# Float16 upper part of the attention weights and the sums' shift on ScalarE, the mixing matmul a step ahead, and the reciprocal last in VectorE's step

## Chip, cores and metric

The kernel runs on one core of a Trainium2 chip. The metric is the time of one execution on the device in microseconds (us); for a version that was run several times it is the median of its runs.

## What is computed

Attention with two mixings over its twelve heads, and a feed-forward part behind it. Cut to what matters (`B, H, S, D = 4, 12, 448, 64`; 1792 tokens, model width 768, inner width 2048):

```python
scores = (1 / sqrt(D)) * q @ k.T                    # each batch and head
scores = einsum('bhij,hg->bgij', scores, w_pre)     # mixing over heads
attn = exp(scores - max(scores, axis=-1))
attn = attn / (sum(attn, axis=-1) + 1e-9)
attn = einsum('bhij,hg->bgij', attn, w_post)        # mixing over heads
x = (attn @ v)                                      # rows: tokens, columns: heads x D
h = x @ w_in
out = (h * 1 / (1 + exp(-1.702 * h))) @ w_out
```

## The kernel before

Large operands are held as two float16 parts, an upper part and what the upper part leaves over (lower part), and a product takes three float16 matmuls. The arithmetic of q, k, v, of the weights and of the attention weights is scaled by powers of two for this.

The program is written out as a main loop of *steps*; a schedule fixed by the program's own order, each engine running its queue in that order. A step treats ten query rows of one batch with all twelve heads, 120 partitions x 448 keys; there are 45 steps for a batch, 180 in all, and behind them the rest of the feed-forward part. In the code `i` is the step.

- `scores` (L221) multiplies q and k for 120 query rows of a pair of heads, `keep_scores` (L231, on ScalarE or VectorE) copies the result out as `sc`, and SP's queue stores it to memory as `sd`. These come some 16 steps ahead (table `at_scores`). `gather(i)` (L247, SP's queue) reads the rows of one step back as `r`, all heads of ten query rows, `AHEAD` steps before.
- `mix(i)` (L257): one matmul in float32 (listed as two records), `mx`, two buffers in PSUM. `peak(i)` (L264, VectorE): the row maximum `nm`. `expo(i)` (L271, ScalarE): `e`, with the row sum `sm`; it comes in the trace with an accumulator read.
- `inverse(i)` (L280, L283, VectorE): `rs`, the scaled inverse of the sum: `sm` has a constant added and is scaled, then the reciprocal. `weigh(i)` (L289, GpSimd): `e` times `rs`, in place. `upper(i)` (L296, VectorE): the float16 part `a1`. `lower(i)` (L302, GpSimd): what is left, `a2`. (The trace names both `a`.)
- `post(i)` (L315 to L317): the second mixing, twelve matmuls into `pp`, `LAG` = 3 steps later. `keep_upper` (L331, ScalarE) and, a step after it, `keep_lower` (L334, VectorE) make the two parts `p`. `context` (L350) multiplies them with v; `x_upper`, `x_lower`, `x_size` make `x`.
- Feed-forward: its 384 *blocks* of six matmuls each (the `quanta`: `hidden`, L522, and `project`, L561) come between the steps' matmuls, 2.15 per step once `x` of the first batch is there. A block's results are taken by `gate` (L540 to L550) and `collect` (L578 to L591), on ScalarE and VectorE, with additions on GpSimd (L588). Matmuls of scores and blocks share three PSUM buffers.
- The weights come as 64-bit floats. `convert` makes sixteen blocks of them into float16 pairs, three parts each: five integer and float operations on VectorE (`magnitude` L423, `least` L427, `shift` L431, `rest` L437, `sign` L443), a sum of squares on ScalarE (L96), a small matmul that adds over partitions (`add_all`, L108), column operations, `w_upper` (L469, ScalarE) and `w_lower` (L472, VectorE), then a store to memory (`wd`). `fetch_w` (L510) reads a block back as `wt` for each use. `q`, `k`, `v` of later batches are treated in a like way (L96, L98, L180 to L188).

What decides where the movable work stands is a count of *tokens* for ScalarE ("A"), VectorE ("D") and GpSimd ("G"): each step adds 4.3 (5.2 when feed-forward blocks run), up to a limit of 3.0, and each operation takes its cost away. A conversion is put into a step only when its engine has tokens left; score copies, some squares and a block's collection go to ScalarE or VectorE, whichever has more. A block of weights has to be converted and stored before feed-forward blocks that read it are put in.

## Time and profile before

| | |
|---|---|
| median of 3 runs | 1174.65 us (1172.79 to 1176.52) |
| profiled execution | 1174.68 us |
| its span, first to last instruction | 1173.0 us |
| TensorE (matmuls) busy | 948.0 us, 81%, mean granted clock 0.886 |
| VectorE busy | 778.0 us, 66% |
| ScalarE busy | 567.3 us, 48% |
| GpSimd busy | 514.5 us, 44% |

The profile is of one execution. Busy time is the time in which an engine ran an instruction. Matmuls overlap each other, so a busy TensorE is not one at its peak. The granted clock is a share of full speed, 2.4 GHz; the lower level is 1.2 GHz, and figures between are means of the two. In rows, PE is TensorE, PEld its weight loads, DVE VectorE, ACT ScalarE, POOL GpSimd, SP the queue that issues most transfers; L is the line of the kernel.

### The profile page before, as it was taken

The page shows a single profiled execution, that of the slowest core. Times are in us where ns is not written, and L with a number is a line of the kernel's source. Part 1 is how long each engine was busy: PE and PEld are TensorE (multiplying, and loading weights), DVE is VectorE, ACT ScalarE, POOL GpSimd, SP SyncE. Part 2 cuts the span into 40 slices and gives each one's busy share as a digit, 9 for nine tenths or more (in the row PEclk, how much of TensorE's full clock was granted, in tenths as well). Part 3 has the DMA queues.
Part 4 walks back from the last instruction along what each step waited for, and adds up shares of the span by engine and source line. Part 5 has one row for each costly group of instructions (what it writes and reads, how often), then busy time and mean ns, then how long its engine had stood idle before and what let it go on. Part 6 is the DMA issues. An engine that isn't in the chain of part 4 may idle for free.

```text
span 1173.0 us, 21128 instructions
## 1 busy us (share of the span) xinstructions
PE 948.0 (81%) x7768; PEld 554.8 (47%) x7768; DVE 778.0 (66%) x1855; ACT 567.3 (48%) x1284; POOL 514.5 (44%) x463
## 2 busy tenths in 40 slices
PE   2557576685778987776659499899999999999998
PEld 1234344353445544443435256465555566555554
DVE  5788778778787878775875477555666566433333
ACT  4444654554546645643544355555544555332322
POOL 0355436545534556454643236455554456320111
PEclk9776768677689998987869799899999999999999
DMA  6766676655747756465644674644655532324332
GB/s 192 226 194 196 229 235 196 217 177 167 216 144 237 231 170 200 142 203 166 201 149 116 208 244 153 194 151 143 196 157 162 177 118 83 101 98 174 108 108 75
DMA packets 67436, 201.02 MB, mean 171 GB/s; under 512 B 7764, under 2 KB 32468, under 8 KB 67332
## 3 DMA queue, kind: packets, MB, share of 16 engines
q1 hardware_dynamic: 66928, 199.59, 53.9%
q8 instruction: 61, 1.00, 0.4%
q14 instruction: 43, 0.35, 0.1%
q10 hardware_dynamic: 404, 0.09, 0.0%
HBM read 143.02 MB, written 56.62 MB: 170 GB/s over the span
## 4 chain that ended last, share of the span: by engine, by line
PE 45%; DVE 29%; ACT 11%; DMA 9%; issue 4%; SPq 1%; ACTq 0%; POOL 0%; DVEq 0%
PE po L561 16%; PE h L522 15%; DVE p L334 5%; PE mx L257 5%; ACT e L271 4%; DVE nm L264 4%; ACT p L331 3%; PE av L350 3%; DVE w_f L437 3%; DVE w_f L443 3%; DMA wt<-wd 2%; DVE w_p L472 2%; DVE w_f L427 2%; DMA wd<-w_p 2%; PE qk L221 2%
## 5 line engine op out<-in xcount | busy, mean ns | idle before, releaser
L302 POOL TENSOR_TENSOR a<-e,a 120x448 f16<-120x448 f32 x180 | 193.4, 1074 | 365.7 <-DVE a L296 307.7
L561 PE MATMUL po<-g,wt 128*128 128x448 f16 x1152 | 248.3, 361 | 30.7 <-DMA wt<-wd 9.9
L289 POOL TENSOR_SCALAR e<-e,rs 120x448 f32<-120x448 f32 x180 | 212.5, 1180 | 127.9 <-DVE rs L283 118.6
L522 PE MATMUL h<-x,wt 128*128 128x448 f16 x1152 | 243.9, 357 | 21.9 <-DMA wt<-wd 15.7
L257 PE MATMUL mx<-r,wa 120*120 120x448 f32 x360 | 200.5, 642 | 35.3 <-ACT e L271 32.3
L271 ACT ACTIVATE e<-mx,nm 120x448 f32<-120x448 f32 x180 | 113.4, 630 | 224.3 <-DVE nm L264 221.4
L561 PEld LDWEIGHTS <-wt 128*128 128x128 f16 x1152 | 111.0, 100 | 151.0 <-issue 55.9
L522 PEld LDWEIGHTS <-wt 128*128 128x128 f16 x1152 | 109.9, 99 | 135.3 <-issue 31.0
L588 POOL TENSOR_TENSOR acc<-acc,pt 128x448 f32<-128x448 f32 x85 | 99.6, 1173 | 139.7 <-ACT pt L585 132.5
L315 PE MATMUL pp<-wp,a 120*112 120x120 f16 x720 | 142.9, 235 | 1.0
L316 PE MATMUL pp<-wp,a 120*112 120x120 f16 x720 | 142.0, 234 | 0.0
L317 PE MATMUL pp<-wp,a 120*112 120x120 f16 x720 | 141.9, 233 | 0.0
L334 DVE TENSOR_TENSOR p<-pp,p 112x480 f16<-112x480 f32 x180 | 116.9, 650 | 15.8 <-ACT p L331 4.0
L264 DVE TENSOR_REDUCE nm<-mx 120x1 f32<-120x448 f32 x180 | 110.8, 615 | 15.9 <-PE mx L257 15.3
L315 PEld LDWEIGHTS <-a 120*112 120x112 f16 x720 | 106.2, 148 | 27.5 <-issue 13.2
L316 PEld LDWEIGHTS <-a 120*112 120x112 f16 x720 | 106.1, 147 | 27.5 <-issue 21.5
L543 DVE SCALAR_TENSOR_TENSOR th<-th,h 128x448 f32<-128x448 f32 x64 | 39.5, 618 | 118.7 <-ACT th L540 118.6
L221 PE MATMUL qk<-kp,qp 64*120 64x448 f16 (+1 forms) x576 | 91.6, 420 | 27.2 <-ACT sc L231 14.2
L331 ACT CAST p<-pp 112x480 f16<-112x480 f32 x180 | 99.4, 552 | 13.7 <-PE pp L317 13.6
L317 PEld LDWEIGHTS <-a 120*112 120x112 f16 x720 | 105.7, 147 | 0.0
L257 PEld LDWEIGHTS mx<-r,wa 120*120 120x120 f32 x360 | 65.0, 206 | 65.8 <-ACT e L271 38.5
L591 DVE SCALAR_TENSOR_TENSOR acc<-po,ct,acc 128x448 f32<-128x448 f32 x83 | 56.6, 682 | 59.2 <-PE po L561 55.9
(128 smaller groups left out, 1177.8 us busy)
## 6 DMA issues: line engine op xcount, KB each, us to landing
wt<-wd SPq DMA_DIRECT2D x64, 768.0 KB, 4.5
r<-sd SPq DMA_DIRECT2D x176, 210.0 KB, 4.3
sd<-sc SPq DMA_DIRECT2D x72, 420.0 KB, 3.6
w<-in_moe_w_in_dram SPq DMA_DIRECT2D x24, 512.0 KB, 9.9
w<-in_moe_w_out_dram SPq DMA_DIRECT2D x24, 512.0 KB, 4.6
wd<-w_p SPq DMA_DIRECT2D x16, 768.0 KB, 5.1
sd<-sc SPq DMA_DIRECT2D x24, 308.0 KB
ka<-in_k_dram SPq DMA_DIRECT2D x12, 448.0 KB, 6.9
```

The costliest lines, as they stand in the source:

```text
L257: nc.tensor.matmul(mx[:K, :S], st["wa", b][:K, :K], row.pop(("r", i))[:K, :], start=True, stop=True)
L264: nc.vector.tensor_reduce(nm[:K], row["mx", i][:K, :S], axis=AX.X, op=ALU.max, negate=True)
L271: nc.scalar.activation(e[:K], row.pop(("mx", i))[:K, :S], AF.Exp, bias=row.pop(("nm", i))[:K, 0:1], scale=1.0, accum_out=sm[:K, 0:1],)
L289: nc.gpsimd.tensor_scalar(e[:K], e[:K], row.pop(("rs", i))[:K, 0:1], 1.0, op0=ALU.mult, op1=ALU.mult)
L302: nc.gpsimd.tensor_tensor(a2[:K], row.pop(("e", i))[:K], row["a1", i][:K], op=ALU.subtract)
L315: nc.tensor.matmul(o, a1[:K, js], wp1[:K, :, :n], start=True, stop=False)
L316: nc.tensor.matmul(o, a1[:K, js], wp2[:K, :, :n], start=False, stop=False)
L317: nc.tensor.matmul(o, a2[:K, js], wp1[:K, :, :n], start=False, stop=True)
L331: nc.scalar.copy(row["p1", i], row["pp", i])
L334: nc.vector.tensor_tensor(mixed_to(i, 2), row.pop(("pp", i)), row.pop(("p1", i)), op=ALU.subtract)
L522: nc.tensor.matmul(h, w[:, i, c, fc * 128:(fc + 1) * 128], x[:, j, c, :], start=(n == 0), stop=(n == len(terms) - 1),)
L561: nc.tensor.matmul(po, w[:, j, fc, e * 128:(e + 1) * 128], g[:, i, fc, :], start=(n == 0), stop=(n == len(terms) - 1),)
```

## The change

The float16 upper part of the attention weights is made by ScalarE from `e` and `rs` (a copy with a scale of one number per partition), and no longer from the weighed `e` by VectorE. GpSimd's weighing writes a tile of its own, `w`, which shares three buffers with `e`. The shift and scaling of the row sum is an activation on ScalarE behind the exponential; VectorE keeps the reciprocal, as the last instruction of its step. The row maximum and the exponential come at the head of a step, the mixing matmul one step earlier, with the gathers, the scores of most chunks and the loads of q and k one step earlier too. The limit of the tokens and some costs change.

```diff
-    AHEAD, LAG = 3, 3
+    AHEAD, LAG = 4, 3
...
+    small = keep.tile([128, 1], F32, name="small")
...
     def expo(i):
...
-        row["e", i], row["sm", i] = e, sm
+        rs = stat.tile([KG, 1], F32, name=f"rs_{i}", tag="rs")
+        nc.scalar.activation(rs[:K], sm[:K], AF.Identity, bias=small[:K, 0:1], scale=2.0 ** -10)
+        row["e", i], row["rs", i] = e, rs
...
     def inverse(i):
...
-        nc.vector.tensor_scalar(
-            rs[:K], row.pop(("sm", i))[:K], 1e-9, 2.0 ** -10, op0=ALU.add, op1=ALU.mult
-        )
-        nc.vector.reciprocal(rs[:K], rs[:K])
+        nc.vector.reciprocal(row["rs", i][:K], row["rs", i][:K])
...
     def weigh(i):
...
-        e = row["e", i]
+        e, w = row["e", i], flow.tile([KG, S], F32, name=f"w_{i}", tag="e", bufs=3)
         nc.gpsimd.tensor_scalar(
-            e[:K], e[:K], row.pop(("rs", i))[:K, 0:1], 1.0, op0=ALU.mult, op1=ALU.mult
+            w[:K], e[:K], row["rs", i][:K, 0:1], 1.0, op0=ALU.mult, op1=ALU.mult
...
     def upper(i):
...
-        nc.vector.tensor_copy(a1[:K], row["e", i][:K])
+        nc.scalar.activation(a1[:K], row.pop(("e", i))[:K], AF.Copy, scale=row.pop(("rs", i))[:K, 0:1])
...
     def lower(i):
...
-            a2[:K], row.pop(("e", i))[:K], row["a1", i][:K], op=ALU.subtract
+            a2[:K], row.pop(("w", i))[:K], row["a1", i][:K], op=ALU.subtract
...
     def refill(t):
...
-            tokens[e] = min(tokens[e] + t, 3.0)
+            tokens[e] = min(tokens[e] + t, 4.5)
...
-        for name, first, ready in (("k", z - 25, z - 16), ("q", z - 23, z - 16), ("v", z - 8, z + LAG + 7)):
+        for name, first, ready in (("k", z - 25, z - 17), ("q", z - 23, z - 17), ("v", z - 8, z + LAG + 7)):
...
+    nc.vector.memset(small, 1e-9 * 2.0 ** -10)
...
-                x = base - (18 if c == NCH - 1 else 16) + 2 * pr if c else base - 10 + pr
+                x = base - (18 if c == NCH - 1 else 17) + 2 * pr if c else base - 11 + pr
...
+    mix(0)
...
         fetch_ahead(i)
-        if i < N:
-            mix(i)
+        if i + 1 < N:
+            mix(i + 1)
         if 0 <= i - 1 < N:
-            inverse(i - 1)
-            spend("D", 0.29)
             weigh(i - 1)
             spend("G", 0.87)
+            upper(i - 1)
+            spend("A", 0.6)
+            lower(i - 1)
+            spend("G", 1.07)
+        if i < N:
+            peak(i)
+            spend("D", 0.62)
+            expo(i)
+            spend("A", 1.02)
...
             keep_lower(i - LAG - 1)
             spend("D", 0.64)
         run_jobs(i)
...
-        if i < N:
-            peak(i)
-            spend("D", 0.62)
-            expo(i)
-            spend("A", 0.82)
-        if 0 <= i - 1 < N:
-            upper(i - 1)
-            spend("D", 0.38)
-            lower(i - 1)
-            spend("G", 1.07)
...
             post(i - LAG)
             keep_upper(i - LAG)
...
         while owed >= 1 and do_quantum(i):
...
+        if i < N:
+            inverse(i)
+            spend("D", 0.15)
```

The built programs show what stands where. First VectorE's queue around two steps in the first stage, where only conversions run beside attention (the numbers are those of buffers). Before, from one sum's shift (L280) to the next:

```order
L280 TENSOR_SCALAR rs_747<-sm_722 120x1
L283 RECIPROCAL rs_747<-rs_747 120x1
L334 TENSOR_TENSOR p_0_0_473<-pp_728,p_0_0_451 112x48x10
L423 TENSOR_SCALAR w_0_f_753<-w_0_64_0_666 128x512
L427 TENSOR_SCALAR w_0_f_753<-w_0_f_753 128x512
L431 TENSOR_SCALAR w_0_f_753<-w_0_f_753 128x512
L437 SCALAR_TENSOR_TENSOR w_0_f_753<-w_0_64_0_666,w_0_f_753 128x512
L264 TENSOR_REDUCE nm_758<-mx_745 120x1
L296 CAST a_9_763<-e_721 120x448
L280 TENSOR_SCALAR rs_798<-sm_761 120x1
```

After (line numbers differ by one or two):

```order
L282 RECIPROCAL rs_743<-rs_743 120x1
L265 TENSOR_REDUCE nm_785<-mx_730 120x1
L333 TENSOR_TENSOR p_0_0_494<-pp_747,p_0_0_462 112x48x10
L422 TENSOR_SCALAR w_0_f_793<-w_0_64_0_705 128x512
L426 TENSOR_SCALAR w_0_f_793<-w_0_f_793 128x512
L430 TENSOR_SCALAR w_0_f_793<-w_0_f_793 128x512
L436 SCALAR_TENSOR_TENSOR w_0_f_793<-w_0_64_0_705,w_0_f_793 128x512
L442 SCALAR_TENSOR_TENSOR w_0_f_793<-w_0_64_0_705,w_0_f_793 128x512
L422 TENSOR_SCALAR w_0_f_801<-w_0_64_1_708 128x512
L282 RECIPROCAL rs_790<-rs_790 120x1
```

The shift and the cast are gone; between the row maximum and the instruction that needs the sum stood one cast, and now stand the `p` subtraction and six conversion operations.

ScalarE's queue at the same place. Before:

```order
L271 ACTIVATE e_721,sm_722<-mx_709,nm_719 120x448
L331 CAST p_0_0_451<-pp_728 112x48x10
L271 ACTIVATE e_760,sm_761<-mx_745,nm_758 120x448
L331 CAST p_0_0_451<-pp_767 112x48x10
L231 COPY sc_2_1_789<-qk_2_1_0_781 120x448
L231 COPY sc_2_1_789<-qk_2_1_1_782 120x448
```

After:

```order
L330 CAST p_0_0_462<-pp_747 112x48x10
L295 ACTIVATE a_9_781<-e_740,rs_743 120x448
L272 ACTIVATE e_787,sm_788<-mx_730,nm_785 120x448
L277 ACTIVATE rs_790<-sm_788,small 120x1
L97 ACTIVATE waste,w_0_m<-w_0_f_793 128x512
L330 CAST p_0_0_462<-pp_803 112x48x10
L295 ACTIVATE a_10_825<-e_787,rs_790 120x448
L272 ACTIVATE e_831,sm_832<-mx_777,nm_829 120x448
```

Each step now opens with the upper part of the step before, then the exponential and the shift; the `p` conversion stands behind the step's squares (`waste`).

TensorE's queue where the main loop begins. Before, one mixing matmul and then the scores of the second chunk; after, two mixing matmuls ahead of the same scores:

```order
L108 MATMUL sums<-mv_305,ones 128x6
L257 MATMUL mx_330<-r_289,wa_209 120x448
L221 LDWEIGHTS qp_0_198
L221 MATMUL qk_1_0_0_337<-kp_0_166,qp_0_198 120x448
L221 LDWEIGHTS qp_0_198
```

```order
L109 MATMUL sums<-mv_309,ones 128x6
L258 MATMUL mx_332<-r_291,wa_211 120x448
L258 MATMUL mx_336<-r_293,wa_211 120x448
L222 LDWEIGHTS qp_0_200
L222 MATMUL qk_1_0_0_345<-kp_0_168,qp_0_200 120x448
```

From there on the mixing matmul of the next step stands at the head of each step's matmuls.

## Rows read from the trace of the kernel before

**Rows 1.** The page's busy time of each engine (share of the span, number of instructions), and TensorE's granted clock in 40 equal slices of the span, in tenths of full speed.
```profile
PE 948.0 (81%) x7768; PEld 554.8 (47%) x7768; DVE 778.0 (66%) x1855; ACT 567.3 (48%) x1284; POOL 514.5 (44%) x463
...
PEclk9776768677689998987869799899999999999999
```

**Rows 2.** Busy time by engine in five stretches of the span (us from its start; number of instructions), with TensorE's granted clock, the DMA engines' share and GB/s: steps 0 to 59, 60 to 89, 90 to 119, 120 to 179, and the rest.
```profile
39.80:338.80 299.00, 201.82 (x1653) 123.77 (x1654) 238.50 (x578) 153.85 (x374) 153.13 (x122) 0.73 0.65 203
338.80:517.10 178.30, 149.74 (x1336) 88.05 (x1334) 142.86 (x339) 104.32 (x243) 95.41 (x78) 0.95 0.62 196
517.10:707.90 190.80, 134.81 (x1120) 78.96 (x1121) 122.66 (x307) 87.12 (x205) 78.73 (x69) 0.82 0.56 176
707.90:1003.00 295.10, 285.23 (x2574) 170.69 (x2573) 185.69 (x441) 156.57 (x347) 154.59 (x158) 0.98 0.50 153
1003.00:1173.00 170.00, 166.24 (x1048) 87.67 (x1046) 67.15 (x131) 50.95 (x85) 29.87 (x27) 1.00 0.33 112
```

**Rows 3.** The instructions of step 10 in order of time (start, duration; in brackets idle time ahead of it and what ended it), VectorE's and then ScalarE's.
```profile
83.65 0.62 DVE L264 TENSOR_REDUCE nm<-mx 120x1 f32<-120x448 f32 x1
84.18 0.38 DVE L296 CAST a<-e 120x448 f16<-120x448 f32 x1
85.14 0.15 DVE L280 TENSOR_SCALAR rs<-sm 120x1 f32<-120x1 f32 x1 [0.57 <-ACT e L271]
85.33 0.16 DVE L283 RECIPROCAL rs<-rs 120x1 f32<-120x1 f32 x1
85.59 0.66 DVE L334 TENSOR_TENSOR p<-pp,p 112x480 f16<-112x480 f32 x1
...
88.34 0.62 DVE L264 TENSOR_REDUCE nm<-mx 120x1 f32<-120x448 f32 x1
...
84.38 0.63 ACT L271 ACTIVATE e<-mx,nm 120x448 f32<-120x448 f32 x1 [3.64 <-DVE nm L264]
```

**Rows 4.** VectorE's waits in stages 1, 2, 3 and 4 (a list for each; us in total, times, longest): that of the sum's shift for ScalarE's exponential.
```profile
DVE rs L280 <- ACT e L271: 30.9, 53, 1.8
...
DVE rs L280 <- ACT e L271: 9.5, 15, 1.5
...
DVE rs L280 <- ACT e L271: 11.0, 19, 0.9
...
DVE rs L280 <- ACT e L271: 12.4, 23, 1.5
```

**Rows 5.** TensorE's waits in stage 3, and the first of its list in stage 4 (us in total, times, longest).
```profile
PE h L522 <- DMA wt<-wd: 15.7, 2, 8.6
PE pp L108 <- DVE p L334: 12.3, 6, 4.8
PE mx L257 <- ACT e L271: 10.9, 7, 3.4
PE po L561 <- DMA wt<-wd: 9.9, 1, 9.9
...
PE po L561 <- ACT sc L231: 3.5, 2, 2.9
```

**Rows 6.** Groups of instructions by line (busy us, mean ns of one; idle time ahead of them and what ended it).
```profile
L289 POOL TENSOR_SCALAR e<-e,rs 120x448 f32<-120x448 f32 x180 | 212.5, 1180 | 127.9 <-DVE rs L283 118.6 <-ACT p L331 4.8 <-ACT x L366 2.5
...
L302 POOL TENSOR_TENSOR a<-e,a 120x448 f16<-120x448 f32 x180 | 193.4, 1074 | 365.7 <-DVE a L296 307.7 <-DVE ct L534 19.4 <-PE pp L317 14.4
...
L331 ACT CAST p<-pp 112x480 f16<-112x480 f32 x180 | 99.4, 552 | 13.7 <-PE pp L317 13.6
...
L296 DVE CAST a<-e 120x448 f16<-120x448 f32 x180 | 79.2, 440 | 6.0 <-POOL e L289 5.6
...
L547 ACT ACTIVATE g<-th,gs 128x448 f16<-128x448 f32 x64 | 43.0, 671 | 47.5 <-DVE th L543 47.5
...
L443 DVE SCALAR_TENSOR_TENSOR w_f<-w,w_f 128x512 int32<-128x512 int32 x48 | 39.6, 824 | 1.0
...
L469 ACT ACTIVATE w_p<-w_f,w_s 128x512 f16<-128x512 f32 x48 | 31.6, 714 | 28.7 <-DVE w_s L460 28.6
...
L280 DVE TENSOR_SCALAR rs<-sm 120x1 f32<-120x1 f32 x180 | 27.0, 150 | 64.0 <-ACT e L271 63.8
...
L231 DVE COPY sc<-qk 120x448 f32<-120x448 f32 (+1 forms) x39 | 23.8, 619 | 32.3 <-PE qk L221 28.7 <-DMA sd<-sc 3.5
L423 DVE TENSOR_SCALAR w_f<-w 128x512 int32<-128x512 int32 x48 | 21.4, 446 | 0.0
...
L98 DVE SCALAR_TENSOR_TENSOR waste<-ka 128x448 bf16<-128x448 f32 x9 | 6.2, 691 | 6.8 <-DMA ka<-in_k_dram 6.7
```

**Rows 7.** From the same view: the accumulator read behind the exponential, and the one activation of a single column, at the program's start.
```profile
L271 ACT ACTIVATION_READ_ACCUMULATOR e<-mx,nm 120x1 f32 x180 | 34.9, 194 | 0.0
...
L758 ACT ACTIVATE warm<-tops 128x1 f32<-128x1 f32 x1 | 0.2, 203 | 0.0
```

**Rows 8.** Line L289, GpSimd's weighing (duration in ns: least, median, most).
```profile
L289 POOL TENSOR_SCALAR e<-e,rs x180: 628/640/4196, 42.2 to 1005.0; 120x448 f32<-120x448 f32 x176, 96x448 f32<-96x448 f32 x4
```

**Rows 9.** Line L257, the mixing matmul and its weight loads: what ended the idle time ahead of them (us, times); behind it TensorE's own wait for the exponential in stage 1 (us in total, times, longest).
```profile
  ACT e L271: 70.8, 45
...
PE mx L257 <- ACT e L271: 18.7, 11, 2.9
```

**Rows 10.** The chain that ended last, its last long piece (start, us, what, number of matmuls: nine blocks of six).
```profile
1159.03 10.23 PE po L561 x54
```

More of the change, by code (lines that the diff above doesn't have):

```diff
@@ L274, in expo @@
         )
-        row["e", i], row["sm", i] = e, sm
+        rs = stat.tile([KG, 1], F32, name=f"rs_{i}", tag="rs")
+        nc.scalar.activation(rs[:K], sm[:K], AF.Identity, bias=small[:K, 0:1], scale=2.0 ** -10)
+        row["e", i], row["rs", i] = e, rs
     def inverse(i):
         K = rows_of(steps[i][1])[1] * H
-        rs = stat.tile([KG, 1], F32, name=f"rs_{i}", tag="rs")
-        nc.vector.tensor_scalar(
-            rs[:K], row.pop(("sm", i))[:K], 1e-9, 2.0 ** -10, op0=ALU.add, op1=ALU.mult
-        )
-        nc.vector.reciprocal(rs[:K], rs[:K])
-        row["rs", i] = rs
+        nc.vector.reciprocal(row["rs", i][:K], row["rs", i][:K])
     def weigh(i):
         K = rows_of(steps[i][1])[1] * H
-        e = row["e", i]
+        e, w = row["e", i], flow.tile([KG, S], F32, name=f"w_{i}", tag="e", bufs=3)
         nc.gpsimd.tensor_scalar(
-            e[:K], e[:K], row.pop(("rs", i))[:K, 0:1], 1.0, op0=ALU.mult, op1=ALU.mult
+            w[:K], e[:K], row["rs", i][:K, 0:1], 1.0, op0=ALU.mult, op1=ALU.mult
         )
+        row["w", i] = w
     def upper(i):
```

## The prediction

> **What bounds the kernel now.** The engines' shares come first: TensorE is busy 948.0 us of 1173.0, VectorE 778.0, ScalarE 567.3, GpSimd 514.5, and TensorE's granted clock is well under full speed in the first half [rows 1]. An average over stages says little, so I cut the span at the starts of VectorE's row maximum `nm` (one per step): steps 0 to 59, 60 to 89, 90 to 119, 120 to 179, and the rest [rows 2]. A step costs 299.0/60 = 4.98 us in stage 1, 178.3/30 = 5.94 in stage 2, 190.8/30 = 6.36 in stage 3 and 295.1/60 = 4.92 in stage 4. VectorE is busy 238.5 of 299.0 us in stage 1 and 142.9 of 178.3 in stage 2. In stage 4 TensorE is busy 285.2 of 295.1 us at clock 0.98, and it is busy nearly throughout the last 170 us, where only the feed-forward part is left.
>
> The instructions of one step of stage 1 tell the rest [rows 3]. VectorE starts `nm` at 83.65 and is then without work for more than 0.1 us only once: the instruction that adds to `sm` waits 0.57 us, because ScalarE could start `e` only after `nm`. ScalarE itself waits 3.64 us. So VectorE's queue is the bound here, and the wait stands in it: 30.9 us in stage 1, then 9.5, 11.0 and 12.4 [rows 4].
>
> Stage 3 is another matter. TensorE is busy only 134.8 of 190.8 us there, and the two longest kinds of wait for the weights' transfer `wt<-wd` cost 15.7 and 9.9 us, beside 12.3 for sums that stand behind VectorE's `p` [rows 5]. Weight blocks are converted by VectorE's spare time, so the feed-forward blocks come only as fast as conversions do.
>
> **The change part by part.** *VectorE, removed.* Per step one cast `a` of 440 ns and one column operation on `sm` of 150 ns [rows 6]: 0.59 us. The reciprocal (0.16 us) stays and moves to the end of the step; what it needs, `sm` shifted on ScalarE, has then been under way since the step's start, so the 0.57 us wait should go. It is hidden by the conversion work between `nm` and the reciprocal, 2.75 us in [rows 3] for `p` and four conversions; without that cover the wait comes back.
>
> *VectorE, added.* With fewer tokens ScalarE passes work on. I counted instructions in the two orders: over the program 50 score copies (619 ns), 24 accumulations, 10 squares and 9 scaled copies (43 at about 691) move to VectorE: 31.0 + 29.7 = 61 us against 106 removed. In stage 1 these are 12 copies and 4 squares (10 us), and conversions come a little earlier (2 `magnitude`, 1 `least`, 1 `shift`, 1 `rest`, 2 `sign`, 3 `w_lower` and a few column operations, at 446 to 824 ns some 7 us): 17 us. In stage 2, 7 copies, 4 accumulations, 3 gate operations and 2 squares (10.5 us), and 20 conversion operations and some column operations more (14 us): 24.5 us.
>
> *ScalarE.* Each step gets the cast with scale and the shift of one column. Neither stands in the trace. The cast is nearest to `g<-th,gs` (same output type, SBUF source, scale from a column: 671 ns) [rows 6]; bounds are the conversions of `p` and of `w_p`, 552 and 714 ns; I take 0.67. The shift is nearest to the one-column activation at the start, 203 ns, or the accumulator read, 194 [rows 7]; the bounds are 0.19 and the 0.55 of a whole conversion of `p`; I take 0.20. That adds 180 x 0.87 = 157 us and takes away about 56 for what is passed on: ScalarE goes to about 668 us. In stage 2, its fullest, it goes from 104.3 to about 130 of 176 us. By the upper bounds (1.26 us per step) it would be 738 in total and some 142 in stage 2. It stays below VectorE's 176, so none of it is in the sum.
>
> The Trainium skill speaks against this move: its page "ScalarE: Activation LUTs", in "Rules for kernel authors", sends multiplies and copies to VectorE rather than ScalarE. The trace agrees on the single operation (440 against 671 ns). By the Trainium skill's same page, in "What ACT_TABLE_LOAD costs", an activation with a column operand takes about 280 ns and 0.833 ns per element, an estimate of 653 ns for the cast and 281 for the shift: 168 us by the page in place of 157.
>
> *GpSimd.* The weighing and the subtraction stay (1180 and 1074 ns); the result gets its own buffer, so `e` and `w` share three. ScalarE's `e` of a step then waits for GpSimd's subtraction of two steps before. That chain is 1.18 + 1.07 us behind the reciprocal, inside a step of over 4 us, so I cost it at nothing. Where weighing is stretched (up to 4.2 us, median 0.64 [rows 8]) the wait can show, some 0.4 us in such a step (4.2 + 1.07 against a step of 4.25 and a cast of 0.67). 24 of its additions go, off the path.
>
> *The mixing matmul a step ahead.* It lets `nm` open VectorE's step without waiting for TensorE. It also has TensorE wait for ScalarE's `e` one step back rather than two; TensorE and its weight loads wait for `e` 70.8 us now, TensorE itself 18.7 in stage 1 and 10.9 in stage 3, while in stage 4 its longest kind of wait is 3.5 us [rows 9, 5]. I take 4 us for it in stage 4. The gathers go one step ahead as well: each keeps its three steps ahead of its matmul, waits for the same earlier matmul to free its buffer, and the scores it reads come a step earlier too. SP's queue holds the same transfers as before, so I cost it at nothing; without that cover a late gather would stop TensorE at the mixing matmul.
>
> *Conversions and the tail.* I counted these in the two orders too. In the one before, 66 of 384 blocks of six feed-forward matmuls are issued when mixing matmul 90 comes, 111 at number 120 and 250 by the last post-mixing; in the one after 68, 127 and 263. The last conversion part comes in step 97 rather than 111. So 14 more blocks fall into stage 3, and 134 - 121 = 13 fewer are left for the end. A block costs 10.23/9 = 1.14 us [rows 10].
>
> The sum. Up to 39.8 us nothing changes.
> - Stage 1: 299.0 - 60 x 0.59 - 30.9 + 17 + 6 (0.1 us per step for new small waits) = 255.7. Bounds 250 (none) to 271 (0.35 per step).
> - Stage 2: 178.3 - 17.7 - 9.5 + 24.5 = 175.6; bounds 168 to 185, as the 26 us of VectorE's other idle time shrink or grow by a third.
> - Stage 3 goes by TensorE: 134.8 + 14 x 1.14 = 150.8 busy. With idle time as small as in stage 4 (a few us) I take 155. Lower bound: stage 4's 4.92 per step with 0.35 blocks fewer, 4.52 x 30 = 136. Upper: 190.8 - 25.6 and a little = 170.
> - Stage 4: 295.1 - 3 x 1.14 (136 blocks instead of 139) + 4 = 296; bounds 290 and 306.
> - Tail: 170 - 13 x 1.14 = 155.2.
>
> 39.8 + 255.7 + 175.6 + 155 + 296 + 155.2 = 1077.3; with the 1.7 us around the span (1174.68 to 1173.0) 1079. The profiled execution's 1174.68 is the median of the runs shown. The bounds add to 1041 and 1129.
>
> **Rivals.**
> *A wait takes the place of the one removed* (0.15). VectorE's `p` subtraction now follows `nm`, and needs ScalarE's `p` cast, which stands behind that step's squares; or the reciprocal comes before the shift is done. For it: the chain between both engines per step stays. Against it: ScalarE waits 3.64 us per step now. Price: the 30.9 + 9.5 us of stages 1 and 2 are not won: 1119.
>
> *ScalarE becomes the bound* (0.08). Its step now begins with 0.67 + 0.63 + 0.19 + 0.20 = 1.7 us behind the reciprocal; where tanh and gate follow, VectorE waits for them and the next step waits for VectorE. With half of the added 0.87 us on the path in the 120 steps of stages 1 to 3 the time is 1079 + 52 = 1131, with four fifths 1163. The Trainium skill's rule on multiplies would make this case.
>
> *Slower* (0.06). TensorE at mixing matmul i+1 waits for `e` of i-1, which follows the accumulation of the last block of TensorE's own step i-2. Accumulation, reciprocal, cast and exponential take 0.68 + 0.16 + 0.67 + 0.82 = 2.3 us, against a TensorE step of 4.9; 2.6 us are spare. If VectorE or ScalarE lags by more in each of the 90 steps of stages 3 and 4, the stall counts in full. The forecast gains 96 us, so it decides from 96/90 = 1.07 us per step on, and at 1.2 us the time is 1079 + 108 = 1187. Against it: stage 4 has VectorE at 63%.
>
> *No change* (0.04): the same with about 1.05 us, or gains of stage 1 given back in stage 3.
>
> *Faster still* (0.05). TensorE's granted clock is 0.73 in stage 1 and 0.82 in stage 3, after its waits, against 0.98 in the well-filled stage 4 [rows 2]. If stage 3 ran at full clock, its 150.8 us would be some 124, with idle time 134: 1079 - 21 = 1058, and with the low bounds of stages 1 and 4 about 1046. The Trainium skill's "TensorE: Matmul & The Clock Gate", in "Part 1", says that the throttled level is the default and activity lifts it; the rows agree.
>
> **How the numbers follow.** My forecast has 0.62 and gives 1079; the range 1040 to 1130 holds it with its bounds, most of the first rival and the faster one, together about 0.8. Within 0.3% (3.5 us) is what a measurement of this kernel cannot tell from no change. Faster: 0.62 + 0.15 + 0.08 + 0.05 = 0.90, of which I leave 0.01 to the rest; same 0.04; slower 0.07.
>
> **What would show it.** Right: no idle time before the reciprocal; `nm` directly behind it; VectorE's step in stage 1 near 4.2 us; no long waits for `wt<-wd` between steps 90 and 120; some 121 blocks behind the last post-mixing; VectorE's total near 732 and ScalarE's near 668. Wrong: VectorE waiting before `p` or the reciprocal in most steps, ScalarE waiting for GpSimd's `a`, TensorE waiting for `e` in stage 4, or stage 3 still above 170 us.

## The result, and the profile after

The changed kernel takes 1133.66 us (median; 1132.17 to 1135.40), the one before 1174.39 beside it: the ratio is 0.965, interval 0.963 to 0.967. It is faster by 41 us. The forecast was 1079, a gain of 96, and the time lies 4 us above the upper end of the range: the sign was right, and the gain was forecast more than twice too large.

The page of the changed kernel, and the busy time in the stretches of [rows 2], with stage 4 and the tail as one (the engines' order is TensorE, its weight loads, VectorE, ScalarE, GpSimd; then granted clock, DMA share, GB/s):

```profile
PE 935.0 (83%) x7768; PEld 546.7 (48%) x7768; DVE 740.1 (65%) x1599; ACT 675.7 (60%) x1541; POOL 428.5 (38%) x439
...
38.96:320.23 281.27, 196.35 (x1643) 120.99 (x1643) 228.99 (x493) 196.65 (x479) 119.07 (x121) 0.76 0.69 219
320.23:519.81 199.58, 159.51 (x1337) 91.79 (x1336) 152.90 (x326) 132.09 (x305) 84.90 (x77) 0.94 0.62 199
519.81:685.90 166.09, 136.17 (x1188) 78.90 (x1186) 104.39 (x236) 99.65 (x231) 65.19 (x71) 0.94 0.56 179
685.90:1131.70 445.80, 432.63 (x3562) 248.88 (x3560) 232.67 (x486) 232.80 (x497) 156.63 (x162) 1.00 0.44 140
```

Against the sum of the forecast, whose terms for stage 4 and the tail are added here:

| us | before | forecast | after | after - forecast |
|---|---|---|---|---|
| up to the first step | 39.8 | 39.8 | 39.0 | -0.8 |
| stage 1, steps 0 to 59 | 299.0 | 255.7 | 281.3 | +25.6 |
| stage 2, steps 60 to 89 | 178.3 | 175.6 | 199.6 | +24.0 |
| stage 3, steps 90 to 119 | 190.8 | 155 | 166.1 | +11.1 |
| stage 4 and tail | 465.1 | 451.2 | 445.8 | -5.4 |
| span | 1173.0 | 1077.3 | 1131.7 | +54.4 |

All of the miss is in stages 1 to 3. The gain also stands elsewhere than forecast: stage 1 gave 18 us of the 43 expected, stage 2 is 21 us longer than before, and the larger gains are in stages 3 and 4 with the tail (25 and 19 us).

The totals of the engines came close: VectorE 740.1 (forecast 732), ScalarE 675.7 (forecast 668). So most of the time was lost in waits. VectorE's waits in stage 1 (us in total, times, longest), the first two of its list and the one that the change was to remove, and then the first of ScalarE's list there:

```profile
DVE p L333 <- ACT p L330: 12.9, 21, 1.6
DVE sc L232 <- PE qk L222: 12.2, 7, 3.9
...
DVE rs L282 <- ACT rs L277: 2.7, 4, 0.7
...
ACT waste L97 <- DVE w_f L442: 49.3, 25, 3.5
```

The wait for the row sum fell from 30.9 us [rows 4] to 2.7, as forecast. In its place VectorE waits for ScalarE's conversion of `p` and, at the score copies that were passed to it, for TensorE. ScalarE itself stands 49.3 us before a sum of squares (L97), which needs VectorE's last conversion operation.

A step shows how the one follows from the other (start, duration; in brackets the idle time ahead and what ended it; other rows left out):

```profile
206.81 0.69 DVE L442 SCALAR_TENSOR_TENSOR w_f<-w,w_f 128x512 int32<-128x512 int32 x1
207.42 0.15 DVE L282 RECIPROCAL rs<-rs 120x1 f32<-120x1 f32 x1
207.50 0.60 DVE L265 TENSOR_REDUCE nm<-mx 120x1 f32<-120x448 f32 x1
207.54 0.63 ACT L97 ACTIVATE waste<-w_f 128x512 bf16<-128x512 f32 x1 [1.77 <-DVE w_f L442]
...
208.17 0.54 ACT L330 CAST p<-pp 112x480 f16<-112x480 f32 x1
208.61 0.97 ACT L232 COPY sc<-qk 120x448 f32<-120x448 f32 x2
208.74 0.66 DVE L333 TENSOR_TENSOR p<-pp,p 112x480 f16<-112x480 f32 x1 [0.64 <-ACT p L330]
...
209.45 0.69 ACT L295 ACTIVATE a<-e,rs 120x448 f16<-120x448 f32 x1
...
210.02 0.64 ACT L272 ACTIVATE e<-mx,nm 120x448 f32<-120x448 f32 x1
...
210.28 1.26 POOL L301 TENSOR_TENSOR a<-w,a 120x448 f16<-120x448 f32 x1 [1.96 <-issue]
...
210.69 1.40 DVE L436 SCALAR_TENSOR_TENSOR w_f<-w,w_f 128x512 int32<-128x512 int32 x1
```

ScalarE idles 1.77 us until VectorE's `sign` (L442), nearly the last work of VectorE's step, is done. Behind the square stand, in ScalarE's queue, the `p` conversion, two copies, the next upper part and the next exponential. VectorE is meanwhile through `nm` and idles 0.64 us before its own `p` (L333). The two engines take turns where they should run beside each other. The last two rows are a second matter: a `rest` (L436) that takes 1.40 us beside GpSimd's subtraction (L301), where the shortest `rest` of this trace takes 0.68.

The groups that answer to [rows 6] (busy us, mean ns; idle time ahead and what ended it):

```profile
L301 POOL TENSOR_TENSOR a<-w,a 120x448 f16<-120x448 f32 x180 | 228.0, 1267 | 115.7 <-issue 52.8 <-ACT a L295 37.2 <-POOL w L287 15.8
L295 ACT ACTIVATE a<-e,rs 120x448 f16<-120x448 f32 x180 | 120.2, 668 | 87.7 <-DVE rs L282 87.1
L287 POOL TENSOR_SCALAR w<-e,rs 120x448 f32<-120x448 f32 x180 | 117.4, 652 | 397.3 <-DVE rs L282 335.9 <-ACT x L365 14.3 <-ACT p L330 8.4
L333 DVE TENSOR_TENSOR p<-pp,p 112x480 f16<-112x480 f32 x180 | 116.4, 647 | 42.4 <-ACT p L330 42.3
...
L277 ACT ACTIVATE rs<-sm,small 120x1 f32<-120x1 f32 x180 | 53.0, 295 | 5.8
L232 DVE COPY sc<-qk 120x448 f32<-120x448 f32 (+1 forms) x89 | 52.7, 618 | 84.1 <-PE qk L222 80.5 <-DMA sd<-sc 3.5
...
L97 ACT ACTIVATE waste<-w_f 128x512 bf16<-128x512 f32 x48 | 30.2, 628 | 81.4 <-DVE w_f L442 81.2
L282 DVE RECIPROCAL rs<-rs 120x1 f32<-120x1 f32 x180 | 27.7, 154 | 12.4 <-ACT rs L277 12.3
```

GpSimd's weighing fell from 1180 to 652 ns, its subtraction rose from 1074 to 1267. VectorE's idle time at the score copies rose from 32.3 to 84.1 us, at `p` to 42.4.

### The profile page after: what moved, and what is told of

Read it like the earlier page. It is cut to its first block, busy times and chain, and to the rows that moved or that the text cites. A ratio compares the mean times of both kernels' runs of the same rounds, so it can differ in the third digit from the quotient of the medians.

```text
span 1131.7 us, 21046 instructions
## 1 busy us (share of the span) xinstructions
PE 935.0 (83%) x7768; PEld 546.7 (48%) x7768; DVE 740.1 (65%) x1599; ACT 675.7 (60%) x1541; POOL 428.5 (38%) x439
## 4 chain that ended last, share of the span: by engine, by line
PE 48%; DVE 31%; ACT 9%; DMA 6%; issue 5%; SPq 0%; ACTq 0%; DVEq 0%
PE po L560 16%; PE h L521 15%; PE mx L258 6%; DVE p L333 4%; PE av L349 3%; DVE w_f L442 3%; DVE w_f L436 3%; PE qk L222 3%; DVE w_f L426 3%; DVE nm L265 2%; DVE w_p L471 2%; DVE w_f L430 2%; PE pp L314 2%; PE pp L315 2%; PE pp L316 2%
## 5 line engine op out<-in xcount | busy, mean ns | idle before, releaser
L560 PE MATMUL po<-g,wt 128*128 128x448 f16 x1152 | 250.2, 361 | 39.6 <-ACT sc L232 20.7
L301 POOL TENSOR_TENSOR a<-w,a 120x448 f16<-120x448 f32 x180 | 228.0, 1267 | 115.7 <-issue 52.8
L287 POOL TENSOR_SCALAR w<-e,rs 120x448 f32<-120x448 f32 x180 | 117.4, 652 | 397.3 <-DVE rs L282 335.9
L258 PE MATMUL mx<-r,wa 120*120 120x448 f32 x360 | 197.4, 634 | 37.0 <-ACT e L272 32.4
L295 ACT ACTIVATE a<-e,rs 120x448 f16<-120x448 f32 x180 | 120.2, 668 | 87.7 <-DVE rs L282 87.1
L333 DVE TENSOR_TENSOR p<-pp,p 112x480 f16<-112x480 f32 x180 | 116.4, 647 | 42.4 <-ACT p L330 42.3
L314 PE MATMUL pp<-wp,a 120*112 120x120 f16 x720 | 137.3, 229 | 0.0
L315 PE MATMUL pp<-wp,a 120*112 120x120 f16 x720 | 136.5, 228 | 0.0
L316 PE MATMUL pp<-wp,a 120*112 120x120 f16 x720 | 136.3, 228 | 0.0
L587 POOL TENSOR_TENSOR acc<-acc,pt 128x448 f32<-128x448 f32 x61 | 71.9, 1181 | 158.2 <-ACT pt L584 158.2
L315 PEld LDWEIGHTS <-a 120*112 120x112 f16 x720 | 102.5, 142 | 23.0 <-issue 16.0
L314 PEld LDWEIGHTS <-a 120*112 120x112 f16 x720 | 102.2, 142 | 23.5 <-issue 12.5
L232 DVE COPY sc<-qk 120x448 f32<-120x448 f32 (+1 forms) x89 | 52.7, 618 | 84.1 <-PE qk L222 80.5
L590 DVE SCALAR_TENSOR_TENSOR acc<-po,ct,acc 128x448 f32<-128x448 f32 x107 | 72.8, 681 | 48.9 <-PE po L560 47.3
```

The source lines that it names most:

```text
L258: nc.tensor.matmul(mx[:K, :S], st["wa", b][:K, :K], row.pop(("r", i))[:K, :], start=True, stop=True)
L287: nc.gpsimd.tensor_scalar(w[:K], e[:K], row["rs", i][:K, 0:1], 1.0, op0=ALU.mult, op1=ALU.mult)
L295: nc.scalar.activation(a1[:K], row.pop(("e", i))[:K], AF.Copy, scale=row.pop(("rs", i))[:K, 0:1])
L301: nc.gpsimd.tensor_tensor(a2[:K], row.pop(("w", i))[:K], row["a1", i][:K], op=ALU.subtract)
L314: nc.tensor.matmul(o, a1[:K, js], wp1[:K, :, :n], start=True, stop=False)
L315: nc.tensor.matmul(o, a1[:K, js], wp2[:K, :, :n], start=False, stop=False)
```

## The experiments

Each is timed beside the kernel before, whose medians were 1172.25 to 1173.62; the ratios are to those. Where one kernel is set against another with changes, the difference of their medians is given. Times of stages, waits and busy times are those of the one profiled execution of each version.

**b_cap: the kernel before with nothing but the higher limit of the tokens.**

```diff
-            tokens[e] = min(tokens[e] + t, 3.0)
+            tokens[e] = min(tokens[e] + t, 4.5)
```

> The kernel before with one number changed: the limit of the tokens 4.5 in place of 3.0. By the order of its instructions the last weight conversion then comes in step 97 (before: 111) and 121 blocks are left behind the last post-mixing (before: 134), just as in the changed kernel. Theory Q (the moves between engines brought little in steps 0 to 119, since a new wait behind ScalarE's queue took the place of the old one; what was won came from earlier conversions): 1140 to 1155 us, most of the gain. Theory M (the moves brought the gain, and the mixing matmul a step ahead took some of it back): 1160 to 1175 us.

1157.02 us (1156.10 to 1158.39), ratio 0.986 (0.983 to 0.989): between the two ranges expected, so that neither theory holds as a whole. The stretches of stages 1 to 3:

```profile
39.88:354.20 314.32, 201.38 (x1661) 125.40 (x1662) 245.18 (x590) 160.85 (x391) 143.09 (x122) 0.75 0.62 197
354.20:557.60 203.40, 167.13 (x1360) 95.80 (x1359) 151.82 (x352) 116.11 (x270) 97.63 (x83) 0.88 0.59 190
557.60:716.67 159.07, 138.95 (x1196) 81.42 (x1196) 107.14 (x270) 85.62 (x198) 75.26 (x76) 0.96 0.62 197
```

Stage 1 is 15 us longer than before, stage 2 25, stage 3 32 shorter, stage 4 with the tail 27 shorter (438.3). By the program's order the last `w_lower` stands in step 97 and 121 blocks are left behind the last post-mixing, the same numbers as in the changed kernel. So the limit alone is enough for the earlier conversions and the fewer blocks at the end, and they are not free: what stages 3 and 4 win, stages 1 and 2 pay for in large part. Whether VectorE's freed time would bring them without the limit was not run. Beside b_cap, the other edits of the change are worth 23 us.

**u_mix: the changed kernel with the mixing matmul, gathers and scores where they were.**

```diff
-    AHEAD, LAG = 4, 3
+    AHEAD, LAG = 3, 3
...
-    mix(0)
...
-        if i + 1 < N:
-            mix(i + 1)
+        if i < N:
+            mix(i)
```

> The changed kernel with the mixing matmul, the gathers, scores and loads of q and k back where they were (one step later). Theory M (TensorE lost its lead by this part; VectorE's score copies now wait for it): 1100 to 1120 us, and VectorE's waits of copies for TensorE fall from 80 us to below 45. Theory Q: within 8 us of 1134, or slower, as the row maximum at the head of VectorE's step would wait for the mixing matmul.

1171.22 us (1167.84 to 1176.39), ratio 0.999 (0.997 to 1.001): without this part nothing of the gain is left. One group shows the wait that comes in its place:

```profile
L265 DVE TENSOR_REDUCE nm<-mx 120x1 f32<-120x448 f32 x180 | 111.0, 617 | 137.3 <-PE mx L258 136.8
```

In the changed kernel VectorE's row maximum opens its step, directly behind the reciprocal, and waits 8.6 us in all for the mixing matmul. With that matmul in the same step it waits 136.8 us, 0.76 per step on average. The mixing matmul a step ahead is thus what the row maximum's new place needs; what it would bring with the row maximum in its old place was not run.

**u_upper: the changed kernel with the upper part's cast back on VectorE** (from the weighed `w`; the cast and GpSimd's subtraction are issued behind `keep_lower`).

```diff
-        nc.scalar.activation(a1[:K], row.pop(("e", i))[:K], AF.Copy, scale=row.pop(("rs", i))[:K, 0:1])
+        nc.vector.tensor_copy(a1[:K], row["w", i][:K])
```

> The changed kernel with the float16 upper part back on VectorE, made from the weighed tile behind the p subtraction; copies, collections and squares then go back to about the distribution of before (54 score copies on VectorE in place of 89). Theory Q (ScalarE's queue delays VectorE): the waits of VectorE for ScalarE's p conversion shrink, VectorE does 180 casts more and 75 passed-on operations less, net about nothing: 1120 to 1140. Theory M or a plain VectorE bound: slower by 15 to 30 us, 1150 to 1165.

1123.37 us (1121.69 to 1126.38), ratio 0.958 (0.954 to 0.961): 10 us faster than the changed kernel. VectorE has 769.3 us of work in it and ScalarE 616.1. So the move that gives the change its name costs time as the kernel stands, and VectorE's work alone is not the bound: it has 29 us more here.

**sq_early, sq_lag, p_early: the queue between VectorE and ScalarE.** sq_lag lets a square be put into a step only if its block's last conversion operation stands in an earlier one. p_early puts the post-mixing and ScalarE's `p` conversion directly behind the exponential, ahead of the step's squares; the small sums of `add_all` then use the PSUM tile of a step earlier. sq_early has both.

```diff
-            sizes.append(job(first, "A", 0.7, lambda a=a: size(a), after=[(last, 0)]))
+            sizes.append(job(first, "A", 0.7, lambda a=a: size(a), after=[(last, 1)]))
```
```diff
             expo(i)
             spend("A", 1.02)
+        if 0 <= i - LAG < N:
+            post(i - LAG)
+            keep_upper(i - LAG)
+            spend("A", 0.55)
         if 0 <= i - LAG - 1 < N:
             keep_lower(i - LAG - 1)
...
-        if 0 <= i - LAG < N:
-            post(i - LAG)
-            keep_upper(i - LAG)
-            spend("A", 0.55)
```

> The changed kernel with two things moved in ScalarE's queue: the squares of weight parts come one step after the VectorE operation that they need, and the second mixing and the p conversion come directly behind the exponential, ahead of the step's squares. Theory Q (ScalarE stands in its queue for VectorE's last conversion operation of the step, with the p conversion behind it, and VectorE's p subtraction then waits for that): the waits of ScalarE's squares for VectorE (81 us) and of VectorE's p for ScalarE's p (42 us) go to below 15 us each, and the time is 1090 to 1112 us. Theory M: within 8 us of 1134.

> The changed kernel with only the squares of the weight parts moved: one step behind the VectorE operation that they need. Theory S (ScalarE standing before the square is what holds up the p conversion, the score copies, the next upper part and the next exponential): most of the 33 us that both moves won, 1100 to 1112. Theory P (it is the place of the p conversion, behind the whole of the step's jobs): less than a third, 1124 to 1136.

> The changed kernel with only the second mixing and the p conversion moved, directly behind the exponential and the shift. Theory P: most of the 33 us, 1100 to 1112, and VectorE's waits before p (42 us) go below 15. Theory S: VectorE's waits before p go down, but ScalarE still stands before the squares (81 us), the next upper part and exponential are late, and less than half is won: 1117 to 1132.

sq_early 1100.70 us (1096.23 to 1102.51), ratio 0.939 (0.935 to 0.942); sq_lag 1108.35 (1106.53 to 1111.83), 0.946 (0.943 to 0.949); p_early 1119.86 (1118.22 to 1120.81), 0.955 (0.952 to 0.958). Against the changed kernel that is 33, 25 and 14 us. VectorE's `p` and ScalarE's squares in the three, in this order:

```profile
L333 DVE TENSOR_TENSOR p<-pp,p 112x480 f16<-112x480 f32 x180 | 115.9, 644 | 3.1 <-ACT p L330 3.1
L97 ACT ACTIVATE waste<-w_f 128x512 bf16<-128x512 f32 x48 | 30.1, 627 | 0.2
```
```profile
L333 DVE TENSOR_TENSOR p<-pp,p 112x480 f16<-112x480 f32 x180 | 116.1, 645 | 21.4 <-ACT p L330 21.3
L97 ACT ACTIVATE waste<-w_f 128x512 bf16<-128x512 f32 x48 | 29.5, 615 | 0.2
```
```profile
L333 DVE TENSOR_TENSOR p<-pp,p 112x480 f16<-112x480 f32 x180 | 115.9, 644 | 2.2 <-ACT p L330 2.2
L97 ACT ACTIVATE waste<-w_f 128x512 bf16<-128x512 f32 x48 | 30.2, 630 | 58.4 <-DVE w_f L442 58.3
```

p_early ends VectorE's wait for `p` (42.4 to 2.2 us) and leaves 58.4 of ScalarE's 81.4 before the squares; sq_lag ends ScalarE's wait and leaves 21.4 of VectorE's. The larger part of the loss is ScalarE's standing; in its queue the upper part and the exponential, with which the next step begins, are behind the square too. With both cured, stage 1 takes 260.3 us and stage 2 192.1:

```profile
38.54:298.84 260.30, 184.55 (x1666) 116.50 (x1666) 225.69 (x490) 196.12 (x474) 125.89 (x121) 0.81 0.73 234
298.84:490.94 192.10, 158.31 (x1314) 90.14 (x1312) 155.92 (x328) 131.60 (x301) 89.10 (x79) 0.93 0.63 204
```

**b_cap_sq: the same lag of the squares in b_cap**, to see whether the wait is the change's doing.

```diff
-            tokens[e] = min(tokens[e] + t, 3.0)
+            tokens[e] = min(tokens[e] + t, 4.5)
...
-            sizes.append(job(first, "A", 0.7, lambda a=a: size(a), after=[(last, 0)]))
+            sizes.append(job(first, "A", 0.7, lambda a=a: size(a), after=[(last, 1)]))
```

> The kernel before with the limit of 4.5 (1157 us) and the squares of weight parts one step later, none of the moves between engines. Theory H (before the change ScalarE waited for VectorE's row maximum at the end of each step anyway, so that standing before a square cost nothing): 1150 to 1160. If the squares' place alone makes the difference, the change apart: 1120 to 1140.

1140.49 us (1140.33 to 1143.83), ratio 0.974 (0.972 to 0.977): 17 us faster than b_cap. The same edit brings 25 in the changed kernel. The theory that the squares' place costs next to nothing as long as ScalarE has no upper part and no shift behind it falls: about two thirds of this loss are there with the higher limit and ScalarE's old work. The other third comes with the rest of the change. What the squares' place cost under the old limit was not run.

**smooth4: sq_early with at most four conversion operations in a step.** It tests whether the bursts that the higher limit allows cost stage 2 its time.

```diff
     def run_jobs(i):
+        made = 0
...
+                if j.get("conv") and made >= 4:
+                    continue
...
+                made += 1 if j.get("conv") else 0
```

> The version with both moves (1100.7 us), and no more than four of VectorE's conversion operations put into a step; the limit of 4.5 let six or seven into some steps and none into others. Conversions end one step later, 122 blocks are left at the end in both. Theory B (steps filled in bursts make stage 2 long: a step with six or seven conversions is bound by VectorE and one with none by TensorE): steps 60 to 89 take 175 to 184 us in place of 192, the whole 1082 to 1092. If bursts do not matter: within 4 us of 1100.

1100.15 us (1098.62 to 1100.86), ratio 0.938 (0.936 to 0.941): no difference from sq_early (1100.70). Stage 2 falls by 4.5 us to 187.6, less than the 8 to 17 expected, and stage 1 rises by 3.1 to 263.4. Bursts are not what makes stage 2 long.

**sq_up: sq_early with the cast back on VectorE**, the edit of u_upper in the other surroundings.

> The version with both moves (1100.7 us), and the float16 upper part back on VectorE behind the p subtraction. Theory E (giving this cast to ScalarE cost more than it freed, whatever the order in ScalarE's queue, as in the changed kernel where taking it back won 10 us): 1087 to 1096. Theory Q2 (it cost only because ScalarE's queue stood still; with that cured the cast on ScalarE is worth its place): 1100 to 1112.

1110.83 us (1101.59 to 1112.15), ratio 0.945 (0.940 to 0.951): 10 us slower than sq_early by the medians, though its runs spread, the lowest is near sq_early's median and the two intervals just overlap (sq_early 0.935 to 0.942). With ScalarE's queue standing, the cast on ScalarE costs 10 us; with that cured it gains some 10, less surely. VectorE's busy time differs by 26.7 us between the two (767.9 and 741.2).

**se_shift: sq_early with the shift back on VectorE** (there as the one column operation that it was, ahead of the reciprocal).

> The version with both moves (1100.7 us), with the shift of the row sum back on VectorE directly ahead of the reciprocal, at the step's end. ScalarE loses 180 x 295 ns = 53 us, VectorE gets 180 x 150 ns = 27 us. By the sum of the prediction (VectorE's queue is the path in steps 0 to 119) it is slower by 120 x 0.19 = 20 us, less what ScalarE no longer passes on (16 score copies fewer on VectorE, 10 us): 1105 to 1115. If ScalarE's queue is the nearer bound: 1085 to 1098.

1099.10 us (1098.34 to 1099.67), ratio 0.938 (0.936 to 0.940): no difference from sq_early, and between the two ranges expected. With the 16 score copies that go back to ScalarE counted in, the shift's place neither gains nor costs; the parts were not told apart.

**no_lower: sq_early without GpSimd's subtraction.** The lower part of the attention weights is a tile of zeros set once, so the product with it adds nothing; its matmuls still run.

```diff
-        nc.gpsimd.tensor_tensor(
-            a2[:K], row.pop(("w", i))[:K], row["a1", i][:K], op=ALU.subtract
-        )
-        row["a2", i] = a2
+        row.pop(("w", i))
+        row["a2", i] = a2z
```

> The version with both moves in ScalarE's queue (1100.7 us), with GpSimd's subtraction left out: the lower part of the attention weights is a tile of zeros in every step, so its product is missing from the result. Theory G (GpSimd's subtraction runs beside VectorE's conversions and stretches them; their means stand 0.02 to 0.34 us above their least): the means of the conversion operations fall to within 0.05 us of their least, VectorE's total falls by 15 to 30 us, and the time by 10 to 25, mostly in steps 0 to 99: 1076 to 1091. If it has no price on the path: within 4 us of 1100.

1066.37 us (1064.86 to 1071.50), ratio 0.911 (0.907 to 0.914): 34 us faster than sq_early, more than the 10 to 25 expected. In the profiled executions it is 29 us, of which 13.5 are in stage 1 (246.8) and 14.3 in stage 2 (177.8). VectorE has the same work as in sq_early and is busy 43 us less. The page's engines and two conversion operations, `least` and `sign`, of no_lower and then of sq_early:

```profile
PE 907.2 (85%) x7768; PEld 528.8 (50%) x7768; DVE 697.9 (65%) x1604; ACT 672.0 (63%) x1537; POOL 211.1 (20%) x259
...
L424 DVE TENSOR_SCALAR w_f<-w_f 128x512 f32<-128x512 f32 x48 | 22.1, 460 | 1.2
L440 DVE SCALAR_TENSOR_TENSOR w_f<-w,w_f 128x512 int32<-128x512 int32 x48 | 33.3, 694 | 1.0
```
```profile
PE 924.3 (84%) x7768; PEld 537.4 (49%) x7768; DVE 741.2 (68%) x1603; ACT 672.3 (61%) x1537; POOL 439.3 (40%) x439
...
L426 DVE TENSOR_SCALAR w_f<-w_f 128x512 f32<-128x512 f32 x48 | 36.9, 769 | 1.2
L442 DVE SCALAR_TENSOR_TENSOR w_f<-w,w_f 128x512 int32<-128x512 int32 x48 | 38.7, 807 | 1.0
```

The subtraction stretches VectorE's operations that run beside it: 769 against 460 ns for `least`, 807 against 694 for `sign`; over the five kinds of conversion operation it is 31 of the 43 us. A wait for the subtraction's result is hardly the other reason: in sq_early's trace no idle time of TensorE ends with the subtraction, and ScalarE waits 0.2 us for it. The 34 us stay an upper bound for the stretching, since what else moves with a shorter GpSimd queue was not told apart.

**se_bias: sq_early with score copies given to ScalarE unless VectorE is richer by more than 1.0.** A version that might beat both, from the reading of L232 above.

```diff
-    e = "A" if tokens["A"] >= tokens["D"] else "D"
+    e = "A" if tokens["A"] >= tokens["D"] - 1.0 else "D"
```

> The version with both moves (1100.7 us), with score copies given to ScalarE unless VectorE has over 1.0 token more: 39 copies on VectorE (as before the change) in place of 90. Theory W (copies on VectorE wait in its queue for TensorE, 69 us in all, and hold up the reciprocal): 1085 to 1095, those waits below 35 us. If they wait only where TensorE is the bound anyway, or ScalarE's queue is no better place: within 5 us of 1100, or slower.

1084.71 us (1083.38 to 1086.16), ratio 0.926 (0.924 to 0.928): 16 us faster than sq_early and the fastest version that computes everything, 49 us below the changed kernel. The waits of VectorE's copies for TensorE over the span, in se_bias and in sq_early, and se_bias's engines:

```profile
DVE sc L232 <- PE qk L222: 62.4, 19, 5.5
```
```profile
DVE sc L232 <- PE qk L222: 69.0, 23, 5.5
```
```profile
PE 913.6 (84%) x7768; PEld 531.2 (49%) x7768; DVE 718.6 (66%) x1560; ACT 688.5 (64%) x1580; POOL 424.3 (39%) x433
```

That wait hardly fell. VectorE has 22.6 us less work and ScalarE 16.2 more, so the gain is rather work that was passed to VectorE and need not have been; how much of the 16 us is which was not separated. By stages the gain is plain: stage 1 stays (261.1 against 260.3), with 9 copies on VectorE in place of 23, and stage 2 falls from 192.1 to 181.3, with 3 in place of 11.

## Why the prediction was wrong, step by step

**Bound and direction: right in part.** The wait for the row sum went (63.8 us over the program [rows 6] to 12.3), and the time fell. But VectorE's queue alone does not set stages 1 and 2 of the changed kernel (u_upper), and what stages 3 and 4 gained, the limit of the tokens brings without any of the moves (b_cap).

**"6 us for new small waits": this step failed first, and it cost the most.** VectorE's waits in stages 1 and 2 were not removed but exchanged. In stage 1 VectorE was idle for 60.5 us before; without the 30.9 of the old wait and with 6 of new ones that makes 35.6. It was idle for 52.3: 22.7 us of new waits in place of 6, which is 16.7 of the stage's miss of 25.6. In stage 2 it was idle for 46.7 us where the sum leaves 25.9, 20.7 of 24.0.

I put ScalarE's 3.64 us of idle time per step [rows 3] down as slack. That was the wait of a single step. Over stage 1 of the kernel before (us in total, times, longest) it is 88.5 us, 1.5 per step, and ScalarE already stood before squares:

```profile
ACT e L271 <- DVE nm L264: 88.5, 45, 8.5
ACT waste L96 <- DVE w_f L443: 40.2, 23, 3.4
```

Nor was it all slack: in an in-order queue a square whose input is VectorE's last work of the step holds up everything behind it, and the change had put the next upper part there, ahead of the next exponential. Curing the squares' place and that of the `p` conversion brings 33 us by the medians. Between the two profiled executions it is 37, of which 21.0 are in stage 1 (281.3 to 260.3) and 7.5 in stage 2, and VectorE's idle time in stage 1 falls to 34.6 us, the size that the forecast had. The first rival named one part of this (`p` behind the step's squares; p_early brings 14 us), had 0.15, and gave 1119. The larger part, ScalarE's own standing before the squares (sq_lag, 25 us), was in no rival, though its wait stood in the trace of before. The second rival, ScalarE as the bound, gave 1131, near the time measured, but by another mechanism: ScalarE was idle for 84.6 of the 281.3 us of stage 1, and sq_early with the same work on ScalarE (672 us) is 33 us faster.

**The cast at 0.59 us per step with its column operation: mis-sized.** In [rows 3] `nm` ends at 84.27 (83.65 + 0.62) and the cast, which started at 84.18 and took 0.38 there, at 84.56: it overlaps `nm` and reaches only 0.29 us beyond it. With 0.15 for the column operation that makes 0.44 us per step, an estimate from this one step: 0.15 x 60 = 9 us too much in stage 1, 0.15 x 30 = 4.5 in stage 2. The whole of stage 1 says the same: the two operations had VectorE to themselves for 26.8 us there, 0.45 per step. With 0.44 and without new waits stage 1 comes to 299.0 - 26.4 - 30.9 + 17 = 258.7; sq_early, with the queues cured, measured 260.3. The agreement may hide further terms of both signs, such as the stretched conversions below.

**Stage 2, bound of 185: too low.** (A third of 26 us either way is 167 to 184.) Its 24.5 us of added work were taken each at its duration, and VectorE's other idle time as unchanged. b_cap has the earlier conversions and none of the moves, and is 25 us longer in stage 2, with 9 us more work on VectorE and 16 us more idle time: they cost more there than VectorE's time for them. In the changed kernel 7.5 of the 24.0 us of miss go with the queues (sq_early). Another 10.8 go when ScalarE keeps more score copies (se_bias, which also has six conversion operations fewer in this stage). Leaving out GpSimd's subtraction takes 14.3 off sq_early's stage 2, but the subtraction ran before the change too, so that is more than its part in the miss.

**Earlier conversions: counts right, price and cause not.** Conversions did end in step 97, and stage 3 did fall from 190.8 to 166.1. That the higher limit brings both by itself, with a bill of 15 and 25 us in stages 1 and 2, I had not separated. Stage 3 did not come to go by TensorE either: TensorE is busy for 136.2 of 166.1 us there, where the forecast had 150.8 of 155. Its granted clock is 0.94 in place of 0.82, which makes its work shorter, and it is idle for 30 us; its longest waits are one of 10.6 us for a score copy on ScalarE and one of 6.7 for the weights' transfer.

**GpSimd at nothing: wrong.** I checked only whether its chain is late. It is not late (ScalarE's `e` waits 0.3 us for the subtraction). Its price is on VectorE: the five kinds of conversion operation went, by the groups by line, from 446, 594, 515, 769 and 824 ns (the first and the last in [rows 6]) to 494, 691, 554, 821 and 862; that is 274 ns for a part of a block and 13 us for the 48 parts, which the sum did not have. Before, the weighing was the longer of GpSimd's two (1180 ns; 652 now). By the Trainium skill's "SBUF — State Buffer", in "Who interferes with whom", VectorE and GpSimd share one pair of ports, and this pair is an exclusive lock; a VectorE instruction contends for it with GpSimd's reads when it has two inputs in SBUF, or when it runs in a mode that uses both ports. The rows of the step above would fit blocking (`rest`, with two inputs, 1.40 us and 0.68 at the least; the subtraction 1.26 and 1.03 at the least), and no run here shows the lock itself.

**Mixing ahead: priced on one side only.** I had entered its cost, TensorE's wait for `e`, as 4 us in stage 4. That wait in stage 1 (18.7 us before [rows 9]) and in stage 4 of the changed kernel:

```profile
PE mx L258 <- ACT e L272: 29.8, 24, 4.9
...
PE mx L258 <- ACT e L272: 0.5, 1, 0.5
```

It grew in stage 1 and not in stage 4. The benefit, that `nm` at the head of VectorE's step need not wait for TensorE, stood in the forecast as given and without a price; without it the whole gain is gone (u_mix, 38 us).

**ScalarE: sum near, one size wrong.** The cast took 668 ns for 0.67. The shift took 295 for my 0.20, 17 us over 180 steps, within its bounds; putting it back made no difference (se_shift). By the Trainium skill's "ScalarE: Activation LUTs", in "What ACT_TABLE_LOAD costs", the estimates were 653 and 281 ns; the trace agrees with both within 5%, and for the shift better than with my nearest rows. The rule in the same page's "Rules for kernel authors" names `mul` among the operations for VectorE and does not name copies; the cast with a scale is a multiply. For it the rule holds in the changed kernel (u_upper is 10 us faster) and not in sq_early (sq_up is some 10 us slower, less surely).

**The rival on the other side** (slower) did not happen: TensorE's 0.5 us in all of stage 4 are far from the 1.07 us per step from which it would have decided.

**Open:** why stage 2 of b_cap grows by 25 us while VectorE gets only 9 us more work there; the lag of the squares takes back 7 (203.4 to 196.0). TensorE's granted clock in that stage fell from 0.95 [rows 2] to 0.88 and its busy time rose from 149.7 to 167.1 us; whether this is a cause or a result no run shows. And the parts of no_lower's 34 us beside the stretched operations.

## What to carry to other kernels

When work moves to an engine with idle time, ask first what ends that idle time: if it is a late product of the bottleneck, everything behind that instruction in the in-order queue may be on the path, and moving the consumer one step later may be worth as much as the move. Price the parts of a change apart: here a scheduler's limit alone made the earlier conversions, the rest lost its gain without the mixing matmul a step ahead, and the move that gave the change its name cost 10 us until the queue was mended. An instruction that overlaps its neighbour is worth only what it reaches beyond it.

## What the hardware showed that was not expected

VectorE's conversion operations took much longer than their shortest only where a GpSimd instruction overlapped them. Of the 240 in the changed kernel 139 had no such overlap, and none of these took more than 430 ns (`magnitude`, `least`, `shift`) or 694 (`rest`, `sign`); the other 101 took 788 and 1060 ns on average. GpSimd's operations stretch as well, and which of its two is the longer changed with the order. `least` (L426) takes 415 ns at the least, 428 in the median and 1257 at the most, GpSimd's subtraction 1030, 1037 and 4876 in the changed kernel. One line's instructions, of the changed kernel and then of sq_early (ns; least, median, most):

```profile
L426 DVE TENSOR_SCALAR w_f<-w_f x48: 415/428/1257, 52.2 to 556.6; 128x512 f32<-128x512 f32 x48
...
L301 POOL TENSOR_TENSOR a<-w,a x180: 1030/1037/4876, 43.4 to 978.2; 120x448 f16<-120x448 f32 x176, 96x448 f16<-96x448 f32 x4
```
```profile
L426 DVE TENSOR_SCALAR w_f<-w_f x48: 414/550/1237, 52.3 to 525.1; 128x512 f32<-128x512 f32 x48
```

In sq_early, the faster kernel, 34 of the 48 `least` meet a GpSimd instruction in place of 23, and the median is 550 ns and not 428. And an activation of a single column costs 295 ns with its scale and a column operand, not the 194 of an accumulator read or the 203 of the one at the program's start [rows 7].
